# One load cut in two, statistics of two tiles exchanged, and written order lists in place of a planner

## The chip, the core and the metric

The kernel runs on one core of one Trainium2 chip. Its time is device microseconds of one execution; the profile is one execution taken by the hardware profiler. The engines are called as in the profile: PE (TensorE matmuls), PEld (TensorE weight loads), DVE (VectorE), ACT (ScalarE), POOL (GpSimd), SP (SyncE, which here issues the DMAs).

## The reference

`x` is 1 x 2048 x 512, `w1` and `w2` are 512 x 512, `w3` is 512 x 1792, `w4` is 1792 x 512, all bf16.

```python
h  = gelu(layernorm(x) @ w1)
c  = D // 4          # four column groups, moved along the sequence by 1, -1, 2, -2 rows, zeros at the ends
hs = concat(h[0:c] down 1, h[c:2c] up 1, h[2c:3c] down 2, h[3c:] up 2) @ w2
x1 = x + hs
return x1 + gelu(layernorm(x1) @ w3) @ w4
```

## The kernel before, in words

The 2048 rows are 16 tiles of 128 rows. Everything stays in SBUF: `x_sb`, the four weights, the transposed normed rows `xnT`, the first activations `hT`, the second ones `h2T`. Numbers q name a tile and its layer norm: q is t for the first norm, 16 + t for the second.

The steps of one tile have names that the text uses. **Statistics**: either `bnst` and `bnag` on DVE (L432, L434), or `sum` and `ssq` on ACT with small `mean`, `msq`, `vpe` on DVE (L411 to L428); the table `STAT_ACT` says which. The second norm's sum comes out of the DVE instruction that makes x1. **rstd** is on POOL (L439). **norm** (L448, L461, L470, L473) is on the engine that `NORM` says, DVE where it says nothing; on ACT and POOL it needs `nmr` first (L466). Tile 0 is only centered, in two halves `norm0_0` and `norm0_1`; its rstd is applied in the gelu (`gelur0`). **tp**: the transpose, for tiles 0 to 7 of the first norm on PE (L506) with an eviction `ev` (L514), for the rest a transposing DMA on SP's queue (L479). **up1** (w1, L642; tile 0 as `rows0_0` and `rows0_1`, L544, with a transpose `th0` and eviction `evh0` back), **mix** (w2 with the row shifts, L697), **x1** (the residual add, L709 or L713), **up2** (w3, L642, blocks named by their first column group), **gelu** (L657), **down** (w4, L731), **res** (L739), **out_dma** (L742).

PSUM has three pairs of banks, `y_ps`, for up1, up2 and the `ty` and `sa` transposes, and two single banks, `o_ps`, for `mix`, `down`, `th` and the `tp` transposes. A step that takes a bank waits for the reader of the step that had it two steps (pair: three steps) before.

Each engine runs its own instructions in program order. PE's order is written in `SCRIPT`. The order on SP, ACT, DVE and POOL is found when the program is built: `order()` gives each operation a due time, worked back from PE's order with the durations written at each `add`, and `place()` walks through a model of engines and queues and takes on each engine what is ready and due first. `LOADS` fixes the order of the loads. The operations that `place()` starts before `ENTRY` are emitted ahead of the entry barrier.

Nine matmuls on zeros (`warm1`, L756) run while the first loads are under way. Only semaphore waits tie the engines together; `emit` derives them from the operations' reads and writes.

Of the kernel before, what the change touches and what calls it, by code (L numbers as in the profile page):

```python
# [6 lines left out]
P = 128  # L7
# [7 lines left out]
class Op:  # L15


    def __init__(self, name, eng, fn, reads, writes, dur, queue):
        self.name, self.eng, self.fn = name, eng, fn
        self.reads, self.writes = list(reads), list(writes)  # L20
        self.dur, self.queue = dur, queue
        self.idx = 0
        self.descs = 8.0
        self.prio = 1e9
        self.first = None

class Program:

    HOP = {"pe": 200.0, "dve": 155.0, "act": 220.0, "pool": 120.0, "sp": 70.0}
    LOOK = {"dve": 300.0, "act": 300.0}
    DUE = 179877.0
    BEGIN = {"sp": 30.0, "act": 150.0, "pe": 400.0, "dve": 150.0, "pool": 450.0}
    ENTRY = 1900.0
    COLD, RESTART = 4300.0, 800.0
    RING = 150.0
    LAG = {"load": 750, "tp": 350}

    def __init__(self):  # L40
        self.ops = []
        self.lines = []

    def add(self, eng, name, fn, reads=(), writes=(), dur=100.0, queue=None):
        op = Op(name, eng, fn, reads, writes, dur, queue)
        op.idx = len(self.ops)
        self.ops.append(op)
        return op

    def line(self, names):  # L50

        self.lines.append(list(names))

    def order(self):
# [25 lines left out]
        order_only = set()  # L80
        for names in self.lines:
            for a, b in zip(names, names[1:]):
                assert named[a].eng == named[b].eng, (a, b)
                order_only.add((named[a].idx, named[b].idx))
        last = None
        pe_pos = 0
        for op in self.ops:
            if op.eng == "pe":
                if last is not None:
                    preds[op.idx].add(last.idx)  # L90
                last = op
                op.prio = pe_pos
                pe_pos += 1
        order_only = {(a, b) for a, b in order_only if a not in preds[b]}
        for a, b in order_only:
            preds[b].add(a)
        succs = [set() for _ in self.ops]
        for i, d in enumerate(preds):
            for j in d:
                succs[j].add(i)  # L100
        left = [len(s) for s in succs]
        stack = [i for i, n in enumerate(left) if n == 0]
        seen = 0
        while stack:
            i = stack.pop()
            seen += 1
            for j in preds[i]:
                if self.ops[j].eng != "pe":
                    self.ops[j].prio = min(self.ops[j].prio, self.ops[i].prio)
                left[j] -= 1  # L110
                if left[j] == 0:
                    stack.append(j)
        assert seen == len(self.ops), "cycle"
        if self.DUE:

            topo, left = [], [len(d) for d in preds]
            stack = [i for i, n in enumerate(left) if n == 0]
            while stack:
                i = stack.pop()
                topo.append(i)  # L120
                for j in succs[i]:
                    left[j] -= 1
                    if left[j] == 0:
                        stack.append(j)
            due, t = {}, self.DUE
            for op in self.ops:
                if op.eng == "pe" and not op.name.startswith("warm"):
                    due[op.idx] = t
                    t += op.dur
            for i in reversed(topo):  # L130
                op = self.ops[i]
                late = due.get(i, 1e9)
                for j in succs[i]:
                    o = self.ops[j]
                    hop = 70.0 if op.queue else (self.HOP[op.eng] if o.eng != op.eng else 120.0)
                    work = (2300.0 if op.queue == "tp" else op.dur + 1850.0) if op.queue else op.dur
                    late = min(late, o.prio - hop - work)
                op.prio = late
        for op in self.ops:
            op.prio += BIAS.get(op.name, 0.0)  # L140
            if op.first is not None:
                op.prio = op.first
        for names in self.lines:
            for a, b in reversed(list(zip(names, names[1:]))):
                named[a].prio = min(named[a].prio, named[b].prio - 1e-3)

        self.preds = preds
        out = self.place(succs, order_only)
        for a, b in order_only:
            preds[b].discard(a)  # L150
        return out

    def place(self, succs, order_only):

        npend = [len(d) for d in self.preds]
        ready = [0.0] * len(self.ops)
        cands = {e: [] for e in ENGINES}
        for op in self.ops:
            if npend[op.idx] == 0:
                cands[op.eng].append(op)  # L160
        free = dict(self.BEGIN)
        rings = {"sp": [], "act": []}
        fed = {}
        clock = moved = last = turned = self.total = 0.0
        out = []

        def finish(limit):
            nonlocal clock
            while True:
                heads = {e: r[0] for e, r in rings.items() if r}  # L170
                if not heads:
                    return None
                live = [e for e in heads if heads[e][0] <= clock]
                later = min([h[0] for h in heads.values() if h[0] > clock], default=1e18)
                if not live:
                    if later > limit:
                        return None
                    clock = later
                    continue
                first = min(live, key=lambda e: heads[e][1])  # L180
                step = heads[first][1] * len(live)
                ends = clock + step <= min(later, limit)
                if not ends:
                    step = min(later, limit) - clock
                for e in live:
                    heads[e][1] -= step / len(live)
                clock += step
                if ends:
                    return rings[first].pop(0)[2]
                if clock >= limit:  # L190
                    return None

        def release(op, o, at):
            npend[o.idx] -= 1
            if at is not None:
                ready[o.idx] = max(ready[o.idx], at)
            if npend[o.idx] == 0:
                cands[o.eng].append(o)

        def land(op):  # L200
            nonlocal moved, last, turned
            if op.queue == "tp":
                turned = max(clock + 500.0, op.start + 2450.0, last + 500.0, turned + 480.0)
                at = turned + self.LAG["tp"]
            elif op.name.startswith("out"):
                at = clock + 300.0
                self.total = max(self.total, at)
            else:
                moved += op.dur
                at = clock + 600.0 + min(600.0, 0.3 * moved) + (600.0 if op.dur > 1400.0 else 0.0)  # L210
                at += 50.0 if moved <= 1200.0 else self.LAG["load"] - 300.0 if moved <= 4000.0 else self.LAG["load"] if moved <= 11000.0 else self.LAG["load"] + 650.0
            if op.queue != "tp":
                last = max(last, at)
            op.landed = at
            for j in succs[op.idx]:
                if (op.idx, j) not in order_only:
                    release(op, self.ops[j], at + 30.0)

        while len(out) < len(self.ops):
            while True:  # L220
                best = None
                for e in ENGINES:
                    if cands[e]:
                        t = max(free[e], min(ready[o.idx] for o in cands[e]))
                        if best is None or t < best[0]:
                            best = (t, e)
                op = finish(best[0] if best else 1e17)
                if op is None:
                    break
                land(op)  # L230
            t, e = best
            look = self.LOOK.get(e, 1.0)
            op = min((o for o in cands[e] if ready[o.idx] <= t + look), key=lambda o: (o.prio, o.idx))
            cands[e].remove(op)
# [674 lines left out]
```

## Time and profile before

| | |
|---|---|
| three runs | 134.98, 135.43, 135.43 us; median 135.43 |
| span of the profiled execution | 133.7 us (its whole time is not given; the runs lie 1.3 to 1.7 above its span) |
| busy | PE 130.6, PEld 71.8, ACT 56.0, DVE 50.9, POOL 30.9 us |
| chain that ended last | PE 94% of the span, DMA 2%, DVE 2% |
| loads | x0-1 issued at 0.08 us, landed 2.8 later; x2 issued at 0.59, landed 2.6 later |
| transposing DMAs | 24, median 2.5 us to landing, 2.4 to 7.0 |
| waits of DVE for the first load | 2.5 us |

The span runs from the first to the last instruction. A line of the timeline or of a group names engine, line of the code, operation, output and input; "x4" counts instructions; brackets give idle time ahead of the engine and what ended it. In a view by stretches each engine has its busy time, then comes the granted PE clock, the DMA share and GB/s. A matmul's end is modelled, and a few per cent of matmul records are missing.

### The profile page before, as it was taken

What the parts mean: (1) busy time and instruction counts of PE and PEld (TensorE: products, weight loads), DVE (VectorE), ACT (ScalarE), POOL (GpSimd) and SP (SyncE); (2) the same over time, 40 slices, a digit from 0 to 9 for tenths busy, and PEclk for the clock granted to TensorE, in tenths of its full rate; (3) what the DMA queues carried; (4) which work ended last, traced back from release to release, by engine and by line L of the source; (5) the groups of instructions that cost most, each with busy time, mean ns of one, the idle gap of its engine ahead of it and who ended that gap; (6) DMA issues with size and microseconds to landing.
All of it is one profiled execution on the core that took longest, in us unless ns stands there. A gap on an engine that the chain in (4) does not pass through costs nothing.

```text
span 133.7 us, 2004 instructions
## 1 busy us (share of the span) xinstructions
PE 130.6 (98%) x776; PEld 71.8 (54%) x789; DVE 50.9 (38%) x138; ACT 56.0 (42%) x89; POOL 30.9 (23%) x69
## 2 busy tenths in 40 slices
PE   8999999999999999999999999999999999999994
PEld 3488768874488444444444444444444444444464
DVE  1899998887550830052260003322220000232223
ACT  5699998858657155520025553000006663000000
POOL 2447567696544120012022003100000000000000
PEclk9999999999999999999999999999999999999999
DMA  4999966745442991002211000311111000111112
GB/s 134 329 349 401 237 150 95 83 89 107 98 99 49 295 329 40 0 0 43 77 42 39 0 0 0 78 39 44 39 42 37 0 0 0 39 44 39 39 39 78
DMA packets 21305, 12.19 MB, mean 91 GB/s; under 512 B 13872, under 2 KB 20784, under 8 KB 21296
## 3 DMA queue, kind: packets, MB, share of 16 engines
q1 hardware_dynamic: 20864, 11.93, 32.7%
q10 hardware_dynamic: 432, 0.13, 0.4%
q8 instruction: 6, 0.10, 0.3%
q14 instruction: 3, 0.02, 0.1%
HBM read 6.82 MB, written 2.10 MB: 67 GB/s over the span
## 4 chain that ended last, share of the span: by engine, by line
PE 94%; DMA 2%; DVE 2%; issue 1%; SPq 0%
PE y_ps L642 46%; PE o_ps L731 36%; PE o_ps L697 10%; DMA x_sb<-in_x_dram 2%; PE y_ps L506 1%; DVE st L432 1%; PE y_ps L544 1%; DVE xn_buf L448 0%; DVE xn_buf L461 0%; DVE o_sb L739 0%; PE o_ps L610 0%; DVE mv L434 0%; SPq L894 0%
## 5 line engine op out<-in xcount | busy, mean ns | idle before, releaser
L642 PE MATMUL y_ps<-xnT,w_sb 128*128 128x512 bf16 (+2 forms) x421 | 63.6, 308 | 0.2
L642 PEld LDWEIGHTS y_ps<-xnT,w_sb 128*128 128x128 bf16 x424 | 38.4, 98 | 24.6 <-DVE mv L434 0.2
L731 PE MATMUL o_ps<-w_sb,h2T 128*128 128x512 bf16 (+3 forms) x248 | 48.7, 355 | 0.2
L657 ACT ACTIVATE h2T<-y_ps 128x1024 bf16<-128x1024 f32 (+1 forms) x29 | 28.6, 993 | 47.2 <-PE y_ps L642 47.1
L731 PEld LDWEIGHTS o_ps<-w_sb,h2T 128*128 128x128 bf16 x252 | 23.6, 98 | 25.2
L739 DVE TENSOR_TENSOR o_sb<-o_ps,x_sb 128x512 bf16<-128x512 f32 (+3 forms) x18 | 11.4, 632 | 45.7 <-PE o_ps L731 45.7
L439 POOL TENSOR_TENSOR rstd<-mv,neghalf 128x1 f32<-128x1 f32 x20 | 11.1, 553 | 35.1 <-DVE mv L434 30.1
L697 PE MATMUL o_ps<-w_sb,hT 128*128 128x512 bf16 x58 | 14.8, 379 | 0.3
L432 DVE BATCH_NORM_STATS2 st<-x_sb 128x6 f32<-128x512 bf16 x20 | 13.5, 676 | 2.6 <-DMA x_sb<-in_x_dram 2.5
L713 DVE TENSOR_TENSOR x_sb<-o_ps,x_sb 128x512 bf16<-128x512 f32 x10 | 6.8, 677 | 14.8 <-PE o_ps L697 14.8
L439 POOL TENSOR_TENSOR rstd<-vpe,neghalf 128x1 f32<-128x1 f32 x12 | 6.7, 558 | 15.6 <-DVE vpe L428 15.5
L473 POOL TENSOR_SCALAR xn_buf<-x_sb,rstd,nmr 128x512 bf16<-128x512 bf16 x12 | 9.2, 764 | 1.0 <-DVE nmr L466 0.4
L657 ACT ACTIVATE hT<-y_ps 128x512 bf16<-128x512 f32 (+1 forms) x10 | 8.1, 806 | 3.1 <-PE y_ps L642 2.9
L697 PEld LDWEIGHTS o_ps<-w_sb,hT 128*128 128x128 bf16 x64 | 6.1, 98 | 5.7
L709 DVE SCALAR_TENSOR_TENSOR x_sb<-o_ps,x_sb 128x512 bf16<-128x512 f32 x6 | 4.1, 681 | 12.1 <-PE o_ps L697 12.1
L416 ACT ACTIVATE junk<-x_sb 128x512 bf16<-128x512 bf16 x12 | 7.5, 622 | 2.1 <-DVE x_sb L709 2.0
L461 DVE TENSOR_SCALAR xn_buf<-x_sb,mv,rstd 128x512 bf16<-128x512 bf16 x13 | 6.1, 471 | 2.7 <-POOL rstd L439 2.0
L470 ACT ACTIVATE xn_buf<-x_sb,nmr,rstd 128x512 bf16<-128x512 bf16 x6 | 4.9, 813 | 0.5 <-POOL nmr L466 0.4
L756 PE MATMUL o_ps<-zeros 128*128 128x512 bf16 x9 | 4.0, 631 | 0.4 <-DVE zeros L363 0.4
L411 ACT ACTIVATE junk<-x_sb 128x512 bf16<-128x512 bf16 x6 | 3.7, 624 | 1.2 <-DMA x_sb<-in_x_dram 1.2
L434 DVE BATCH_NORM_AGGREGATE mv<-st 128x2 f32<-128x9 f32 x20 | 3.8, 192 | 0.3
L506 PE MATMUL y_ps<-ident,xn_buf 128*128 128x128 bf16 x32 | 3.4, 236 | 0.2 <-DVE xn_buf L461 0.2
(34 smaller groups left out, 28.7 us busy)
## 6 DMA issues: line engine op xcount, KB each, us to landing
out_dram<-o_sb SPq DMA_DIRECT2D x15, 128.0 KB, 1.7
w_sb<-in_w_dram SPq DMA_DIRECT2D x1, 1792.0 KB, 10.9
w_sb<-in_w_dram SPq DMA_DIRECT2D x2, 896.0 KB, 6.2
x_sb<-in_x_dram SPq DMA_DIRECT2D x4, 256.0 KB, 3.6
w_sb<-in_w_dram SPq DMA_DIRECT2D x4, 256.0 KB, 4.3
x_sb<-in_x_dram SPq DMA_DIRECT2D x5, 128.0 KB, 4.5
x_sb<-in_x_dram SPq DMA_DIRECT2D x1, 384.0 KB, 5.7
xnT<-xn_buf SPq DMA_TRANSPOSE x24, 2.5
```

Source lines behind the costliest of these rows:

```text
L416: (lambda d: (lambda e: e.activation(d, src, ACT_F.Square, accum_out=sums[:, q, 1:2])))(junk[:, b, :]),
L432: pg.add("dve", f"bnst{q}", lambda e: e.bn_stats(st9[:, q, 0:6], src), reads=rs, writes=[(("st", q), 0)], dur=605)
L439: lambda e: e.tensor_tensor(col(rstd), var, neghalf[:], ALU.pow),
L461: lambda e: e.tensor_scalar(dst, src, mv[:, q, 0:1], rstd[:, q : q + 1], ALU.subtract, ALU.mult),
L470: f = lambda e: e.activation(dst, src, ACT_F.Identity, bias=nmr[:, q : q + 1], scale=rstd[:, q : q + 1])
L473: f = lambda e: e.tensor_scalar(dst, src, rstd[:, q : q + 1], nmr[:, q : q + 1], ALU.mult, ALU.add)
L642: ins = e.matmul(y_ps[:, p, W * i : W * (i + 1)], wsb[:, dc, P * fc : P * (fc + 1)], src[:, dc, P * t0 : P * t0 + W], start=(dc == 0), sto ...
L657: (lambda d, s: (lambda e: e.activation(d, s, ACT_F.Gelu_apprx_tanh)))(dst, ysrc),
L697: ins = e.matmul(dst, hT[:, j, c0 : c0 + P], w2_sb[:, j, :], start=(j == order[0]), stop=(j == order[-1]))
L713: f = lambda e: e.tensor_tensor(x1_sb[:, t, :], dst, x_sb[:, t, :], ALU.add)
L731: ins = e.matmul(dst, h2T[:, fc, P * t : P * (t + 1)], w4_sb[:, fc, cs], start=(fc == 0), stop=(fc == FC - 1))
L739: (lambda d, c: (lambda e: e.tensor_tensor(o_sb[:, oi, c], d, x1_sb[:, t, c], ALU.add)))(dst, cs),
```

## The change

The planner (`place()`, due times, durations, `BIAS`) goes; the order of SP, ACT, DVE and POOL stands in `ORDER`, one list for each, and `AHEAD` names what is emitted ahead of the entry barrier. `SCRIPT` can name single blocks of up1 and up2. The order itself is other than before: x0 is loaded alone and x1 and x2 together; tile 0's statistics are bnst and bnag on DVE, tile 2's are sum and ssq on ACT; other tiles change engine in `NORM`, `EVAC`, `STAT_ACT`, `NMR` and `HEV`; up2 blocks stand between mix, up1 and down steps; the transposes of tiles 1, 6 and 7 use single banks.

```diff
 GROUPS = {1: (1, 1, 1, 1, 1, 2, 1, 2, 2, 4), 2: (2, 2, 4, 4, 4)}
-NORM = {5: "act", 6: "pool", 7: "act", 9: "pool", 10: "pool", 11: "act", 12: "act", 15: "pool", 18: "act", 19: "pool", 20: "act", 21: "pool", 23: "pool", 25: "pool", 26: "pool", 28: "pool", 30: "pool", 31: "pool"}
-EVAC = {1: "both", 2: "dve", 4: "dve", 5: "dve", 6: "both", 7: "dve", 8: "dve", ...}
-STAT_ACT = (0, 5, 7, 9, 10, 12, 19, 21, 23, 24, 25, 31)
+NORM = {4: "pool", 6: "pool", 9: "act", 10: "act", 18: "act", 19: "pool", 20: "act", 25: "pool", 26: "act", 29: "pool", 31: "act"}
+EVAC = {0: "dve", 1: "dve", 2: "both", 3: "act", 4: "dve", 5: "act", 6: "dve", 7: "dve"}
+STAT_ACT = (2, 7, 9, 10, 12, 16, 17, 18, 19, 21, 25, 28)
-HEV = {0: "dve", ...}
+HEV = {0: "act"}
-NMR = {0: "pool", 1: "pool", 3: "pool", 5: "pool", ...}
+NMR = {4: "pool", 6: "pool", 18: "pool", 20: "pool", 25: "pool", 26: "pool"}
 LOADS = """
-x0-1 x2 tp2 w1a w1b x3 x4-5 w2b w2a tp5 x6 tp6 x7 x8-10 tp4 w3 x12-13 tp0 x11 tp17 x14-15 tp26 tp5 w4a tp3
-w4b
+x0 x1-2 w1a w1b x3 x4-5 w2b w2a x6 x7 x8-10 w3 x12-13 x11 x14-15 w4a w4b
 """
+AHEAD = "zeros trip0 trip1 neghalf ident0 epsc pad0 ident1 pad1 warm_gelu warm1 dma_x0 dma_x1 dma_w1a dma_w1b".split()
 SCRIPT = """
-warm:9 sa:0 sb:0 ty:1 ra:0 rb:0 ty:2 up1:1 th:0 up1:2 mix:0 ty:3 mix:1 ty:4 up1:3 ty:5 up1:4 ty:6 mix:2
-up1:5 ty:7 mix:3 up1:6 mix:5 mix:4 up2:0 up1:7 mix:6 up1:8 mix:7-8 up1:9 mix:10 mix:9 up2:1 mix:13 mix:11
-up2:2 mix:14 down:2 down:1 down:0 mix:12 up2:3 mix:15 down:3 down:5 down:7 down:4 down:6 down:10 up2:4
-down:8 down:11 down:9 down:12-15
+warm:9 sa:0 sb:0 ra:0 tp:1 rb:0 ty:2 up1:1.0 th:0 up1:2.0 ty:3 mix:0 mix:1 ty:4 up1:3.0 up1:4.0 tp:6 ty:5
+mix:2 tp:7 up1:5.0 mix:3 up1:6.0 mix:5 mix:4 mix:6 up2:0.0 up2:0.4 up2:0.8 up1:7.0 up1:8.0 mix:7 mix:8
+up2:0.12 mix:10 mix:9 up1:9.0 up2:1.0 up1:9.2 up2:1.4 mix:13 mix:11 up2:1.8 mix:12 up2:2.0 up2:1.12 up2:2.2
+up2:2.4 down:1 up2:2.6 mix:14 up2:2.8 up2:2.10 down:0 mix:15 up2:3.0 up2:3.2 up2:3.4 down:2 up2:2.12 down:3
...
 """
+ORDER = {
+    "sp": """
+dma_x0 dma_x1 dma_w1a dma_w1b dma_x3 dma_x4 dma_w2b dma_w2a dma_x6 dma_x7 dma_x8 dma_x11 dma_w3 dma_x12 tp16
+tp17 dma_x14 tp8 tp9 tp10 tp11 tp18 tp13 tp12 tp14 tp15 tp19 tp23 tp22 tp21 tp20 dma_w4b dma_w4a tp28 tp25
+tp26 out_dma1_0 tp24 tp30 tp27 out_dma3_0 tp31 out_dma5_0 ...
+""",
+    "act": """
+warm_gelu sum2 ssq2 gelur0 ev2act gelu1_1_0 evh0 gelu1_2_0 ev3 ssq7 sum7 sum9 ssq16 gelu1_3_0 ssq17 ev5 ssq9
+gelu1_4_0 sum10 ssq10 gelu1_5_0 ssq18 ssq19 gelu1_6_0 norm9 norm18 ssq21 norm10 sum12 ssq12 gelu2_0_0
...
+""",
+    "dve": """
+zeros bnst0 bnag0 bnst1 norm0_0 bnag1 norm0_1 msq2 vpe2 ev0_0 norm1 ev0_1 norm2 ev1 bnst3 ev2dve bnag3 bnst4
+norm3 bnag4 bnst5 bnst6 bnag6 x1_0 bnag5 ev4 msq7 x1_1 mean16 vpe7 norm5 msq16 mean17 msq9 vpe16 ev6 norm7
+msq17 vpe17 norm16 x1_2 ev7 norm17 mean18 vpe9 bnst8 msq10 msq18 bnag8 x1_3 norm8 nmr9 mean19 vpe10 msq19
+vpe19 vpe18 x1_5 nmr10 x1_4 nmr19 mean21 bnst20 x1_6 bnag20 bnst22 bnst11 bnag22 bnag11 bnst13 norm11 msq21
...
+""",
+    "pool": """
+trip0 trip1 neghalf ident0 epsc pad0 ident1 pad1 rstd0 rstd1 rstd2 rstd3 rstd4 nmr4 norm4 rstd6 rstd5 nmr6
+norm6 rstd7 rstd16 rstd17 rstd9 rstd8 rstd10 rstd18 rstd19 nmr18 norm19 ...
+""",
+}
```

For comparison, the order that the planner gave SP was: x0-1, x2, w1a, w1b, x3, x4-5, w2b, w2a, x6, x7, x8-10, w3, x12-13, x11, tp16, tp17, x14-15, tp9, tp8, tp10, tp11, tp12, tp13, tp14, tp15, tp19, tp18, tp21, tp20, tp22, tp23, tp24, tp26, w4a, w4b, tp25, tp27, tp29, tp30, out_dma2, out_dma1, out_dma0, tp28, tp31 and the other writes; and DVE's began with zeros, bnst1, bnag1, norm0_0, norm0_1, bnst2, norm1, bnag2, msq0, vpe0, norm2, ev1dve, bnst3, ev2.

## The prediction

> **What bounds the kernel now.** I read the busy shares first, then TensorE (PE) by stretch of the span, then its timeline, then the DMA queues.
>
> ```profile
> PE 130.6 (98%) x776; PEld 71.8 (54%) x789; DVE 50.9 (38%) x138; ACT 56.0 (42%) x89; POOL 30.9 (23%) x69
> 0.00:5.12 5.12, 4.45 (x13) 1.66 (x14) 2.32 (x9) 3.24 (x8) 1.55 (x13) 1.00 0.62 206
> 5.12:20.00 14.88, 14.72 (x160) 11.24 (x164) 13.75 (x47) 13.73 (x35) 9.34 (x19) 1.00 0.92 288
> 20.00:34.00 14.00, 13.95 (x106) 10.29 (x106) 11.57 (x39) 11.05 (x19) 10.12 (x21) 1.00 0.57 92
> 64.00:132.00 68.00, 67.61 (x337) 32.22 (x341) 12.97 (x25) 15.06 (x16) 3.16 (x6) 1.00 0.11 32
> ```
>
> The first line is the page's, the others the view by stretches: length, then busy time of PE, PEld, DVE, ACT, POOL. From 5.12 us on PE is full. Its leftover of some hundredths is matmul records missing from the trace (a step of four shows three). The timeline has one true PE wait after the warm-up:
>
> ```profile
> 4.24 0.63 PE L506 MATMUL y_ps<-ident,xn_buf 128*128 128x128 bf16 x4
> 5.12 0.49 PE L506 MATMUL y_ps<-ident,xn_buf 128*128 128x128 bf16 x4 [0.25 <-DVE xn_buf L461]
> 31.47 3.62 PE L642 MATMUL y_ps<-xnT,w_sb 128*128 128x512 bf16 x16
> ```
>
> The third line is up1_9, the first block that needs tp15, the last DMA transpose of layer 1; it began on time. From 5.12 to 20 us DVE and ACT are over nine tenths busy too: little room there.
>
> The matmul work is the same after the change: same tiles transposed on PE (0 to 7), same groups, same nine warm-ups. So the end moves only by when dense PE work begins and by new PE waits. The last matmuls, their eviction (0.26) and the final write stay. The span is 133.7; the median 135.43 lies 1.7 above it (the three runs 1.3 to 1.7), and that part is left alone. I add the sum to both.
>
> **The change, part by part.**
>
> *Head.* x0 alone is 128 KB instead of 256. The two load rows, x0-1 and then x2:
>
> ```profile
> DMA to landing us min/median/max: 2.8/2.8/2.8
> DMA to landing us min/median/max: 2.6/2.6/2.6
> ```
>
> Issued at 0.08 and 0.59, they land at 2.85 and 3.16: 128 KB more cost 0.30. So x0 lands at about 2.53 (estimate; between 2.3 and 2.85), and x1-2, the same bytes in total, at 3.16. DVE then runs bnst0 (0.69) to 3.22, bnag0 to 3.45, and, because its list says so, bnst1 (starts 3.36, to 4.05) before norm0_0. Before, norm0_0 began 0.84 after the landing (3.71); now about 1.43 after it: 3.96, to 4.21. So the 0.32 won by the load is given back by the second bnst. PE's warm-up ends at 4.24 in any case. tp0_0 runs at 4.27, tp0_1 at 4.54; ev0_0, now on DVE behind msq2 and vpe2, runs 4.73 to 5.01; rows0_0 starts at 5.07, tp1 (norm1 to 5.43) at 5.5, rows0_1 at 5.73, tp2 at 6.16, up1_1 at 6.4 to 6.5. Before, up1_1 began at 6.54. Head: -0.1, bounds -0.25 and +0.2. It can't be much better: PE's order needs the warm-up, a transpose, an eviction and rows0_0 one after the other, and that alone reaches 5.0.
>
> *Statistics and norms moved.* DVE still has 20 bnst and ACT 12 ssq. POOL norms fall from 12 to 5, DVE gains 7 (0.41 each, 2.9 in all), ACT keeps 6. None of it is on the path unless a norm is late for its transpose. Three are, each followed by its own rows. norm4 now goes to POOL: bnag4 ends 8.45, rstd4 (0.55) 9.09, nmr4 (0.26) 9.45, norm4 (0.76) 10.31, tp4 10.41; PE is free at 10.36: 0.06. norm6 waits for POOL behind norm4, rstd6, rstd5: ends 12.46, tp6 12.56, PE free at 12.43: 0.13. norm5 on DVE meets that POOL norm. What that costs stands in this pair:
>
> ```profile
> 25.42 0.76 POOL L473 TENSOR_SCALAR xn_buf<-x_sb,rstd,nmr 128x512 bf16<-128x512 bf16 x1
> 25.53 0.80 DVE L461 TENSOR_SCALAR xn_buf<-x_sb,mv,rstd 128x512 bf16<-128x512 bf16 x1 [0.24 <-POOL rstd L439]
> ```
>
> The DVE norm took 0.80 instead of 0.41, ending 0.14 after POOL's. vpe7, queued ahead of norm5, would be held likewise (vpe12 took 0.53 instead of 0.16 beside norm10), which pushes norm5 from 12.39 to 12.79 and costs tp5 0.06; msq16 to norm7 behind it shift too, and tp7 has 0.06 to spare. Then mix6, moved ahead of up2_0, needs the bank that x1_5 frees (19.41) when mix4 is just done (19.39): 0.08. Sum 0.33; bounds 0 (all inside my reading error of 0.1 each) and 0.7 (each 0.1 worse).
>
> *PE order.* up2_0 is split: three blocks (1.745 each) before up1_7 and up1_8, the last (0.87) after mix8. mix6 goes first. up1_9_0 came at 31.47; now the same steps stand ahead of it in another order, and mix10 and mix9 (0.86 each) besides: 31.47 + 1.73 + 0.2 = 33.4. up2_3 (due 63.6) needs tp27, which in SP's list stands behind out_dma1, tp24 and tp30: mix14 ends 56.4, x1_14, res1, bnst30, bnag30, rstd30, norm30 to 59.5, tp30 59.7, tp27 61.0, landed 63.5: room 0.1, cost 0 (bounds 0 and 0.3).
>
> *SP's list.* tp18 is put ahead of tp13, tp12, tp14 and tp15, and norm10 comes later: ACT does gelu1_6, norm9, norm18 (waits for nmr18 until 20.2), ssq21, then norm10 to 22.47; tp10 is issued at 22.57 (before: 21.12). tp11 waits for norm11 (24.24): 24.34. Then tp18, 13, 12, 14, 15 at SP's pace of 1.31 each: tp15 at 30.89, landed 2.45 later at 33.34. Due 33.4: room 0.05. Before, tp15 landed at 31.16, due 31.47: room 0.3, with a block of 1.0 already paid. That block is the row the forecast rests on:
>
> ```profile
> GB/s 0 3 148 225 215 212 69 2 0 109 20 176 210 201 176 35 0 0 0 7 9 9 10 10 12 0 60 188 217 218 173 19 0 0 0 137 224 215 215 82
> q8 instruction: 1, 0.02, 1.5%
> DMA to landing us min/median/max: 4.2/4.2/4.2
> L479 SPq DMA_TRANSPOSE xnT<-xn_buf x1: 2272/2272/2272, 23.7 to 23.7; - x1
> DMA to landing us min/median/max: 2.5/2.5/2.5
> ```
>
> The first two lines are the DMA view of 22 to 28 us: one 16 KB instruction packet (queue 8; 1.5% of 16 engines for 6 us is 1.4 us, and it stands at 23.43 to 24.90), and from 24.3 to 25.9 nothing else moves. The others are SP's transposes one by one: tp11, issued 22.36, landed after 4.2; tp12's issue took 2.27 instead of 1.27, so tp13 came at 26.01 instead of 25.00; from then on 2.5 again. The six such packets start when PE and PEld have done 256, 424, 669, 933, 1167 and 1419 instructions, mostly some 250 apart, so I take them as PE's. In the new PE order the second one comes at the same instruction, mix6 and 33 matmuls of up2_0 on: 20.3 + 33 x 0.109 = 23.9, with tp10 in flight and the queue without a gap until tp15. Price: up to 1.0, all of it visible, since the room is 0.05: up1_8 (needs tp11, due 27.3) would wait some 0.4, up1_9 the rest. The average packet is shorter (0.3% of 16 engines over the span, over six: 1.07), so bounds are 0 and 1.3; I take 0.8.
>
> [...]
>
> *Rest.* x11 ahead of w3 (128 KB) delays w3 by about 0.3: due at 20.3, landed 16.5 before. The dropped planner and durations issue nothing. The set issued ahead of the entry barrier has the same members. SP still issues 24 transposes; w4 stands behind tp20 at about 40 and is needed at 51. Cost 0; w4's cover is some 3 us.
>
> Sum: -0.1 + 0.33 + 0.8 = +1.0: span 134.7, time 136.4 (+0.75%).
>
> **Rivals.** *The packet costs nothing here* (it falls between two transposes, or is only as long as the shortest): then +0.2, 135.6, not slower by what can be told. For it: the packet of 40.4 to 41.7 stood beside one transpose (issued 40.79, landed after 2.5) and cost it nothing. Against: that transpose was alone; from 22.6 to 33.3 there will be no gap between them. It decides if the delay is below 0.4. [...] *A second choke*: a further packet on the transposes (queue 14 moved two of 8 KB at 20.1 and 21.1, where tp9 and tp8 took 4.0 and 3.9) or up2_3 on tp27: +0.5 more, 136.9. *Faster*: x0's landing shortens the start and no wait is real: rows0_0 at 5.0 and dense from there gives -0.25, 135.2. Over 0.5% (0.68) it would have to start some 0.4 before ev0_0 can be done; I see no way. That the lists don't do what they say is hardly possible: they are the program order.
>
> **Numbers.** 0.5% (0.68 us) is about what a measurement of this kernel can tell from no change; the runs before differ by 0.45. Chances: forecast 0.52 (of which 0.08 has a delay so small that the total stays under 0.68), harmless packet 0.30, second choke 0.13, start gain 0.05 (0.03 of it beyond 0.5%, for what I can't see). Slower 0.44 + 0.13 = 0.57; same 0.08 + 0.30 + 0.02 = 0.4; faster 0.03. The range takes the harmless case with 0.3 of spread below, and the second choke's middle: 135.3 to 136.9; the forecast's own is 135.9 to 136.8.
>
> **What would show it.** Right: in the new PE timeline gaps before up1_8 and up1_9 (27 to 35 us) ended by a transpose, one SP transpose taking over 2 us to issue near 24, and up1_1 at 6.4 to 6.5. Wrong: PE dense through 27 to 35 with all transposes landing in 2.5 (then 135.6); or first dense work before 5.0.

## The result, and the profile after

The changed kernel took 137.24 us (median of six executions, 136.5 to 137.75) beside 135.43: 1.0134 times the kernel before (95% interval 1.0109 to 1.016). The forecast was 136.4, at most 136.9: the direction held, the time lies above the range. Its profiled execution took 137.26, with a span of 135.4; before, the span was 133.7. In all that follows "outside the span" means an execution's time less its span. One execution of e4_packet_early, two of e9_room and one of e12_before_loads (its profiled one) were slow, above all the others of their kernel; times, spans and ratios leave them out, and that profile is not read.

The busy line of the page, and PE by stretch (length, then busy time of PE, PEld, DVE, ACT, POOL):

```profile
PE 131.6 (97%) x776; PEld 71.3 (53%) x789; DVE 50.7 (37%) x147; ACT 54.2 (40%) x86; POOL 24.3 (18%) x55
5.12:20.00 14.88, 14.51 (x153) 10.56 (x156) 13.59 (x53) 12.72 (x32) 8.55 (x16) 1.00 0.81 279
20.00:34.00 14.00, 13.95 (x107) 10.40 (x108) 11.87 (x36) 9.66 (x16) 7.11 (x14) 1.00 0.46 86
34.00:36.00 2.00, 1.50 (x8) 0.56 (x7) 1.97 (x7) 0.00 (x0) 0.61 (x1) 1.00 0.39 78
64.00:132.00 68.00, 67.68 (x319) 31.47 (x323) 11.25 (x18) 15.74 (x16) 0.55 (x1) 1.00 0.11 31
```

POOL has 14 instructions fewer (55 for 69); that will matter at the very end. PE is full from 64 us on, as before. What it lost lies ahead of 20 us and between 34 and 36. PE's timeline at these places (start, length, engine, line, operation; in brackets the idle time ahead and what ended it):

```profile
4.35 0.59 PE L344 MATMUL y_ps<-ident,xn_buf 128*128 128x128 bf16 x4
5.27 1.01 PE L381 MATMUL y_ps<-w_sb,xnT 128*128 128x512 bf16 x2 [0.34 <-DVE xnT L352]
7.03 1.07 PE L477 MATMUL y_ps<-xnT,w_sb 128*128 128x128 bf16 x16
34.88 5.36 PE L477 MATMUL y_ps<-xnT,w_sb 128*128 128x512 bf16 x31 [0.49 <-DMA xnT<-xn_buf]
```

The first three are tp0, rows0_0 and up1_1. Up1_1 came at 7.03; before, its row was

```profile
6.54 1.06 PE L642 MATMUL y_ps<-xnT,w_sb 128*128 128x128 bf16 x16
```

The fourth is up1_9, waiting for tp15: 34.88, before 31.47 with 1.73 of mix steps less ahead of it. The chain of waits (start, length, piece) passes through that wait:

```profile
30.96 0.70 DVE x_sb L547
31.66 0.51 SPq L317
32.22 2.53 DMA xnT<-xn_buf
34.88 4.07 PE y_ps L477 x26
```

SP's transposes fill their queue up to 32.22, the last lands 2.5 later, and PE stands. How the queue came to be late is seen in the DMA view of 24 to 30 us and in tp11's own row:

```profile
GB/s 0 20 184 225 215 188 42 0 0 109 0 0 0 0 61 140 205 222 177 68 26 24 5 0 1 0 0 0 123 224 215 217 93 4 0 0 12 174 222 220
q8 instruction: 1, 0.02, 1.0%
L317 SPq DMA_TRANSPOSE xnT<-xn_buf x1: 1849/1849/1849, 25.1 to 25.1; - x1
```

The instruction packet (queue 8) ran from 25.48 to 26.48. Behind the packet's own column (the 109) the GB/s row is empty up to 26.1; tp11's issue took 1.85 instead of 1.27, and its landing 3.0 instead of 2.5. PE's spacing shows 0.13 of wait before up1_8 and 0.66 before up1_9.

### The profile page after: what moved, and what is told of

It reads as the page before. It is cut to its first block, busy times and chain, and to the rows that moved or that the text cites. A ratio compares the mean times of both kernels' runs of the same rounds, so it can differ in the third digit from the quotient of the medians.

```text
span 135.4 us, 1992 instructions
## 1 busy us (share of the span) xinstructions
PE 131.6 (97%) x776; PEld 71.3 (53%) x789; DVE 50.7 (37%) x147; ACT 54.2 (40%) x86; POOL 24.3 (18%) x55
## 4 chain that ended last, share of the span: by engine, by line
PE 91%; DMA 4%; issue 1%; ACT 1%; DVE 1%; SPq 1%; DVEq 0%
PE y_ps L477 45%; PE o_ps L565 36%; PE o_ps L531 8%; DMA x_sb<-in_x_dram 2%; DMA xnT<-xn_buf 2%; PE y_ps L381 1%; PE y_ps L344 1%; PE o_ps L344 1%; ACT junk L250 1%; DVE x_sb L547 1%; ACT junk L255 0%; SPq L317 0%; SPq L224 0%; DVE o_sb L573 0%; PE o_ps L446 0%
## 5 line engine op out<-in xcount | busy, mean ns | idle before, releaser
L477 PE MATMUL y_ps<-xnT,w_sb 128*128 128x512 bf16 (+2 forms) x417 | 64.4, 307 | 0.9 <-DMA xnT<-xn_buf 0.5
L565 PE MATMUL o_ps<-w_sb,h2T 128*128 128x512 bf16 (+3 forms) x250 | 49.8, 355 | 0.1
L492 ACT ACTIVATE h2T<-y_ps 128x1024 bf16<-128x1024 f32 (+1 forms) x29 | 27.8, 991 | 48.0 <-PE y_ps L477 48.0
L547 DVE TENSOR_TENSOR x_sb<-o_ps,x_sb 128x512 bf16<-128x512 f32 x9 | 6.1, 685 | 17.3 <-PE o_ps L531 17.2
L299 DVE TENSOR_SCALAR xn_buf<-x_sb,mv,rstd 128x512 bf16<-128x512 bf16 x20 | 8.0, 404 | 2.9 <-POOL rstd L278 2.9
L255 ACT ACTIVATE junk<-x_sb 128x512 bf16<-128x512 bf16 x12 | 7.5, 623 | 0.8 <-DVE x_sb L543 0.8
L543 DVE SCALAR_TENSOR_TENSOR x_sb<-o_ps,x_sb 128x512 bf16<-128x512 f32 x7 | 4.8, 685 | 0.2 <-PE o_ps L531 0.2
L311 POOL TENSOR_SCALAR xn_buf<-x_sb,rstd,nmr 128x512 bf16<-128x512 bf16 x5 | 3.8, 763 | 1.0 <-DVE nmr L304 0.4
L250 ACT ACTIVATE junk<-x_sb 128x512 bf16<-128x512 bf16 x5 | 3.1, 624 | 1.6 <-DMA x_sb<-in_x_dram 1.6
L267 DVE SCALAR_TENSOR_TENSOR vpe<-sums,mv 128x1 f32<-128x1 f32 x12 | 2.1, 182 | 2.4 <-ACT junk L255 2.3
```

Source lines behind the costliest of these rows:

```text
L255: (lambda d: (lambda e: e.activation(d, src, ACT_F.Square, accum_out=sums[:, q, 1:2])))(junk[:, b, :]),
L299: lambda e: e.tensor_scalar(dst, src, mv[:, q, 0:1], rstd[:, q : q + 1], ALU.subtract, ALU.mult),
L477: ins = e.matmul(y_ps[:, p, W * i : W * (i + 1)], wsb[:, dc, P * fc : P * (fc + 1)], src[:, dc, P * t0 : P * t0 + W], start=(dc == 0), sto ...
L492: (lambda d, s: (lambda e: e.activation(d, s, ACT_F.Gelu_apprx_tanh)))(dst, ysrc),
L543: f = lambda e: e.scalar_tensor_tensor(x1_sb[:, t, :], dst, 1.0, x_sb[:, t, :], ALU.mult, ALU.add, accum_out=sums[:, NT + t, 0:1])
L547: f = lambda e: e.tensor_tensor(x1_sb[:, t, :], dst, x_sb[:, t, :], ALU.add)
```

## The experiments

Times are medians; the ratio is to the kernel before on the same chip, with its 95% interval; "span" is the median of the executions' spans, "outside" their range outside the span. The kernel before had 135.42 to 135.50 beside all of them, with spans of 134.1 (134.2 beside e5 to e8) and 1.3 to 1.4 outside.

| run | kernel | time | ratio | span | outside |
|---|---|---|---|---|---|
| (first) | after | 137.24 | 1.0134 [1.0109, 1.016] | 135.4 | 1.50 to 2.01 |
| e11_after_again | after | 136.65 | 1.0082 [1.0067, 1.0097] | 135.15 | 1.47 to 1.53 |
| e1_tp18_late | after | 136.85 | 1.0109 [1.0085, 1.0132] | 135.2 | 1.49 to 1.91 |
| e4_packet_early | after | 136.67 | 1.0095 [1.0062, 1.0129] | 135.2 | 1.46 to 2.05 |
| e5_pool_spare | after | 136.65 | 1.0084 [1.0058, 1.011] | 135.3 | 1.33 to 1.38 |
| e9_room | after | 135.80 | 1.0027 [1.0014, 1.0041] | 134.45 | 1.30 to 1.37 |
| e8_norm46 | after | 136.36 | 1.0076 [1.0051, 1.01] | 134.8 | 1.51 to 1.57 |
| e2_head_back | after | 136.76 | 1.0099 [1.0071, 1.0128] | 135.2 | 1.45 to 1.91 |
| e16_head_back_room | after | 135.83 | 1.0033 [1.0018, 1.0048] | 134.5 | 1.29 to 1.40 |
| e3_fill | after | 136.49 | 1.0071 [1.0045, 1.0098] | 134.6 | 1.46 to 2.01 |
| e13_norm0_first | after | 136.73 | 1.0107 [1.0085, 1.0128] | 135.2 | 1.45 to 2.01 |
| e17_start_free | after | 136.95 | 1.0119 [1.0095, 1.0142] | 135.6 | 1.31 to 1.41 |
| e7_all | after | 136.79 | 1.0106 [1.0074, 1.0139] | 135.25 | 1.52 to 1.60 |
| e10_room_all | after | 136.07 | 1.0042 [1.0029, 1.0054] | 134.55 | 1.47 to 1.60 |
| e14_norm0_room | after | 135.83 | 1.0038 [1.0022, 1.0055] | 134.3 | 1.48 to 1.58 |
| e18_all_mended | after | 136.55 | 1.0091 [1.0072, 1.0111] | 135.0 | 1.50 to 1.57 |
| e6_before_fill | before | 135.34 | 0.9994 [0.9978, 1.001] | 133.95 | 1.30 to 1.41 |
| e12_before_loads | before | 136.20 | 1.0055 [1.0036, 1.0073] | 134.9 | 1.30 to 1.37 |
| e15_before_loads_again | before | 135.88 | 1.003 [1.0018, 1.0042] | 134.5 | 1.29 to 1.38 |

The second column names the kernel that was edited. No version beat the kernel before.

### The packet and the transposes: e1, e4, e9

e1 moves tp18 behind the transposes of layer 1:

```diff
-tp17 dma_x14 tp8 tp9 tp10 tp11 tp18 tp13 tp12 tp14 tp15 tp19
+tp17 dma_x14 tp8 tp9 tp10 tp11 tp13 tp12 tp14 tp15 tp18 tp19
```

> One move in SP's list of the changed kernel: tp18 goes from between tp11 and tp13 to behind tp15. Theory (tp15 has no room, and the blocked issue of tp11 shows through it): tp15 lands 1.31 us earlier, the 0.66 us before up1_9 goes, up2_1 waits some 0.1 for tp19 instead, time 0.5 to 0.6 us below the changed kernel (about 136.7). Rival (the place of the wait just moves to up2_1, because tp18 and tp19 are as late as tp15 was): no change within 0.2.

up1_9 no longer waited, but the queue was as late as before and the next reader paid, up2_1, on a transpose further on:

```profile
34.12 1.89 PE L477 MATMUL y_ps<-xnT,w_sb 128*128 128x512 bf16 x8
36.54 3.63 PE L477 MATMUL y_ps<-xnT,w_sb 128*128 128x256 bf16 x24 [0.52 <-DMA xnT<-xn_buf]
```

The span did not move (135.2): the rival was right. tp18's place is not the cause; it only chose who waits.

e4 moves the packet. Its place seems to go by the count of PE's instructions: where the six packets of queue 8 begin, PE and PEld have started 247, 437, 728, 916, 1166 and 1421 of them in after, 256, 424, 669, 933, 1167 and 1419 in before. So the nine warm-up matmuls of 512 columns become 36 of 128, the same work in 54 more PE and PEld instructions:

```diff
-            rows = zeros[:].unsqueeze(1).to_broadcast([P, 4, P])
+            rows = zeros[:]
...
-                for _ in range(n):
-                    ins = e.matmul(o_ps[:, b, :], zeros[:], rows, start=True, stop=True)
+                for _ in range(4 * n):
+                    ins = e.matmul(o_ps[:, b, 0:P], zeros[:], rows, start=True, stop=True)
```

> The nine 128x512 matmuls on zeros become 36 of 128x128: same time, but 54 more TensorE instructions ahead of everything, so the second 16 KB instruction packet (25.48 to 26.48 in the changed kernel) should come some 27 matmuls, 2.9 us, earlier, at about 22.5, where no transposing DMA moves data. Theory (the packet is what blocks tp11's issue for 0.57): tp11's issue takes 1.27 again, tp15 lands 0.6 earlier, the wait before up1_9 falls from 0.66 to about 0.1, time 0.5 to 0.6 below the changed kernel (about 136.7). Rival (tp11 is held by something of its own, such as its input or the queue): the packet moves and tp11's issue stays near 1.85, no change in time.

The six packets came at 12.64, 21.04, 37.96, 65.12, 86.72 and 114.64 us (after: 14.49, 25.48, 46.9, 66.12, 93.2, 120.8): earlier, by 1.0 to 8.9. tp11, issued at 24.8, took 1.19 and landed after 2.7, and up1_9 came without a bracket:

```profile
L317 SPq DMA_TRANSPOSE xnT<-xn_buf x1: 1192/1192/1192, 24.8 to 24.8; - x1
33.96 6.23 PE L477 MATMUL y_ps<-xnT,w_sb 128*128 128x512 bf16 x40
```

In that profile the waits before up1_8 and up1_9 fell from 0.79 to 0.12, at a span of 134.5. A rival falls with it: an 8 KB packet of queue 14 also ran beside the transposes (from 26.17 in after), and in e4 it ran at the same place (25.89) while they kept their pace. The spans of e4's other executions scatter from 134.4 to 135.5, and the median time is not lower than e5's; so e4 shows whose packet it is and what it does, and not the gain in time.

e9 leaves the packet where it is and gives the transposes room, that is, issues them earlier than PE's need of them asks (with 14 spare POOL memsets, below):

```diff
-gelu1_6_0 norm9 norm18 ssq21 norm10 sum12
+gelu1_6_0 norm9 norm10 ssq21 norm18 sum12
...
-nmr19 mean21 bnst20 x1_6 bnag20 bnst22 bnst11 bnag22 bnag11 bnst13 norm11 msq21
+nmr19 mean21 bnst11 bnst20 bnag11 x1_6 bnag20 norm11 bnst22 bnag22 bnst13 msq21
...
-nmr18 norm19 rstd20 rstd11 nmr20
+nmr18 norm19 rstd11 rstd20 nmr20
```

> The kernel after, with 14 spare memsets at the end of POOL's list (by the earlier run with them alone the time outside the span goes back to 1.35) and room for the last transposes of layer 1: ACT does norm10 before norm18, DVE does bnst11, bnag11 and norm11 earlier, POOL rstd11 before rstd20, so that tp10 to tp15 can be issued about 1.4 us earlier. Theory (the wait of 0.79 before up1_8 and up1_9 is there because the packet meets transposes that have no room): tp11 is issued near 23.6, tp15 lands at 33.3 to 33.9 instead of 34.75, up1_9 waits at most 0.3, the span is 134.6 to 134.8, the time about 136.0 (0.7 us below the run with the spare memsets alone). Rival (some other transposing DMA or packet then sets the end, as when tp18 alone was moved): the span stays at 135.2 to 135.5, the time at 136.6.

tp11 was issued at 23.72. The packet (25.61) met it all the same: it landed after 4.1, and tp18's issue behind it took 2.3. tp15 landed at 34.07, and PE did not wait:

```profile
32.48 1.89 PE L534 MATMUL o_ps<-w_sb,hT 128*128 128x512 bf16 x8
34.20 6.02 PE L480 MATMUL y_ps<-xnT,w_sb 128*128 128x512 bf16 x37
```

The span's median fell from e5's 135.3 to 134.45, the time from 136.65 to 135.80. So the packet is a price only where the transposes have no room, and here that price is about 0.8 in time. In the profiles of kernels without that room it varies: the two waits add up to 0.79 in after, 0.57 in e11, 0.52 in e3 and 1.03 in e5.

### Outside the span: e5, e11

```diff
-nmr26 rstd30 rstd31
+nmr26 rstd30 rstd31 spare0 spare1 ... spare13
```

> Fourteen small POOL memsets on a column of their own are added at the end of POOL's list in the changed kernel; nothing reads them and POOL is idle there. In the runs so far the time outside the span is 1.31 to 1.39 us for the kernel before and 1.45 to 2.05 (near 1.5 or near 1.95) for the changed one, whose trace has an 8 KB instruction packet on queue 14 1.8 us after the last instruction; the kernel before has its third such packet at 40.8. The built programs have 78 POOL instructions before, 64 after. Theory (with 14 fewer POOL instructions a block boundary of POOL's stream falls behind the kernel's end, and the end waits for the packet): the packet goes back inside the span, time outside the span 1.31 to 1.4, span unchanged (135.4), time 0.3 to 0.5 below the changed kernel (about 136.8). Rival (the time outside the span has another cause, such as DVE's or ACT's stream): it stays 1.5 to 2.0 and the time stays.

The spare operations are 14 memsets of one column at the end of POOL's list: they do no work that anybody needs. All six executions had 1.33 to 1.38 outside the span, as the kernel before; after had 1.5 or 1.9 to 2.0, nothing between. What stands there is seen in the DMA view from 134 us on, after's first, then e5's (start of the row at 134, 0.125 us a column):

```profile
GB/s 0 3 200 123 3 0 117 80 0 0 0 0 0 0 0 0 0 0 0 0 0 0 0 0 0 66 0 0 0 0 0 0 0 0 0 0 0 0 0 0
q14 instruction: 1, 0.01, 0.4%
```

```profile
GB/s 0 0 120 192 16 0 61 125 11 0 0 0 0 0 0 0 0 0 0 0 0 0 0 0 0 0 0 0 0 0 0 0 0 0 0 0 0 0 0 0
```

After fetches an 8 KB instruction packet on queue 14 at 137.15, 1.75 us behind its last instruction. With the memsets that third packet moved to 48.23, where it lies under other work; before has it at 40.79. Of the profiled executions only after's and e3's have a packet behind the end, and these two had 1.86 and 1.98 outside; the other profiled executions of after and its versions without the memsets had 1.49 to 1.54. So with 14 POOL instructions fewer a fetch is left for the end of the program (137.15 in after, beside 48.23 with the memsets), and where it is seen there the time outside is some 0.6 longer. That the executions with 1.5 have the same fetch, only not recorded, is not shown: the memsets took their 0.15 away too, but e7, e10, e14 and e18, whose third packet lies at 47 to 48 us, have 1.5 all the same.

> The kernel after, unchanged, on the chip of these runs. By what its earlier runs showed: time 137.2 +- 0.3, spans with a median of 135.4, time outside the span between 1.5 and 2.0 and in two clusters. Rival (the difference to the other kernels is one of chips or of hours): 136.7 or less, and 1.35 outside the span.

Between theory and rival: the time was 136.65, the spans 134.9 to 135.3, and all six had 1.5 outside. Of after's twelve executions eight had 1.5 outside and four 1.9 or 2.0. The first measurement had all four; that is two thirds of its distance to this one (0.38 by the medians, out of 0.59).

### The start: e2, e3, e6, e12, e15, e13, e17, e16

e2 puts the start of before into after, with DVE's list, POOL's rstd order and AHEAD to match:

```diff
-x0 x1-2 w1a
+x0-1 x2 w1a
-STAT_ACT = (2, 7, 9, ...)
+STAT_ACT = (0, 7, 9, ...)
-warm:9 sa:0 sb:0 ra:0 tp:1 rb:0 ty:2
+warm:9 sa:0 sb:0 tp:1 ra:0 rb:0 ty:2
```

> The start alone is put back in the changed kernel: loads x0-1 and x2, tile 0's statistics on ACT (sum0, ssq0), tile 1 and 2 on DVE, ev0_0 and ev0_1 on ACT, tp1 ahead of rows0. Theory A (the new start costs 0.5: ev0_0 stands behind ssq2 and vpe2, and TensorE's matmuls stay at half pace until 6.2 instead of 5.35): up1_1 starts near 6.5 instead of 7.03, time 0.5 below the changed kernel (about 136.7). Rival B (when the pace doubles is chance from run to run and not tied to the start): 0.1 to 0.2 below only.

136.76, span 135.2: no lower than after's 135.15 to 135.4 by anything that can be told, where half a microsecond stood in the profile. In e2's profile up1_1 came at 6.75, but up1_8 and up1_9 then waited 0.96 instead of 0.79: what the start wins, the late transposes take back. With them out of the way (e16, the old start and e9's room) it can be read:

> The kernel with room for the transposes and spare POOL memsets, and the start of the kernel before (x0-1 and x2, tile 0's statistics on ACT, its evictions on ACT, tile 1's transpose ahead of rows0_0). Theory (start, small waits, packet and the part outside the span are all): only the small waits of some 0.36 are left over the kernel before: span median 134.3 to 134.5, time 135.6 to 135.8. Rival (the old start doesn't pay in the new order): 135.9 or more, as with room and the new start.

135.83 and a span of 134.5, the same as e9's 135.80 and 134.45, and 0.4 above before's: by time between theory and rival, by span the theory's. So on average the new start costs nothing that can be told in this order, though 0.44 lie between the profiles of e9 and e16 at up1_1 (7.14 and 6.70); in that profile of e9 the second load landed later than in any other with this start (3.83).

A part of such differences is the pace of the matmuls. In after's profile the steps from rows0_0's two matmuls to what follows each were 0.38 and 0.43, from about 6.2 us on they are 0.22. e3 puts one warm-up matmul into the gap before rows0_0, e6 does the same to the kernel before:

```diff
-warm:9 sa:0 sb:0 ra:0 tp:1
+warm:9 sa:0 sb:0 warm:1 ra:0 tp:1
```

> One more matmul on zeros (128x512) is put between tp0_1 and rows0_0 of the changed kernel, in the 0.5 us in which TensorE stands idle there. Theory A (the idle time is why matmuls stay at half pace until 6.2): the pace doubles at about 5.4, rows0_0 takes 0.43 instead of 0.8, time 0.3 to 0.4 below the changed kernel (about 136.9). Rival B (the moment is chance, or counts from the launch): no change within 0.1.

> The kernel before with one more matmul on zeros between tp0_1 and tp1, in its idle 0.45 us; POOL's first constants come in another order, all else as before. Theory A (TensorE's idle time ahead of the first dense step makes the doubling of its pace late in some runs, in both kernels): spans less spread than 133.7 to 134.7, median span 133.7 to 133.9, time 0.2 to 0.4 below the kernel before. Rival B (the moment is chance that idle time doesn't touch, and the 0.75 that the fill won in the changed kernel was something else): same time within 0.1.

e3 had full pace at rows0_0 (5.30) and up1_1 at 6.64, and its span was 134.6. But in its profile tp0's last two matmuls and the filling matmul start 0.07 and 0.06 apart (0.11 in e13, at half pace): the pace was up at 4.68, before the filling had run, so the filling did not bring it; e6 changed nothing; in e10 rows0_0's first step was 0.38 in spite of the filling; and e1 and e13 had full pace at rows0_0 without it. Where a trace has a record of the granted clock from early on, it agrees with the pace: the record begins, at full clock, at 6.17 us in after, 6.36 in e11, 6.38 in e8, 5.88 in e10 and 3.92 in e1, all with the start of after, and at 5.37 in before. (The clock column of the views shows 1.00 ahead of that as well, where the trace has no record.) So the step to full pace lay anywhere from 3.9 to 6.4 us in these profiles; what sets its moment is not shown. In e3's profile, 0.6 below after's, 0.39 are at up1_1 and 0.27 at the transposes; what the lower median comes from stays open.

e12 does the edit of the title's first half alone, in the kernel before; PE's order stays, and the planner makes the other engines' lists anew:

```diff
-x0-1 x2 tp2 w1a
+x0 x1-2 tp2 w1a
-STAT_ACT = (0, 5, 7, ...)
+STAT_ACT = (2, 5, 7, ...)
-EVAC = {1: "both", ...}
+EVAC = {0: "dve", 1: "both", ...}
```

> The kernel before with the first words of the change alone: x0 as a load of its own, x1 and x2 in the next, statistics of tile 0 on DVE, of tile 2 on ACT, the eviction ev0 on DVE; PE's order and the planner stay. Theory (the loss comes from the order lists, not from this): the start moves by -0.1 to +0.3, no new wait after 6 us, 1.35 outside the span, time 135.3 to 135.8. Rival (the loads and statistics themselves cost the loss): 136.2 or more, with the first dense PE work 0.8 later.

> The kernel before with the new loads, statistics and eviction of the start, unchanged from its earlier run. Theory (tile 0's norm waits for the second load, and the evictions of tile 0 and norm1 stand one after the other on DVE): x1-2 lands at 3.2 to 3.5, tile 0's transpose starts 1.25 later, up1_1 at 7.2 to 7.5 beside 6.54 before, no other wait; span median 135.0, time 136.3. Rival (the loss is elsewhere): up1_1 before 6.9 and a wait after 10 us.

136.20 and, repeated, 135.88: by the medians the edit alone costs 0.4 to 0.8 there, with PE's order unchanged. Why it costs that in the order of before and nothing visible in that of after (e9 beside e16) is open. The first theory fell. The repeat's trace shows how (PE, then DVE):

```profile
4.61 0.59 PE L506 MATMUL y_ps<-ident,xn_buf 128*128 128x128 bf16 x4
7.01 1.06 PE L642 MATMUL y_ps<-xnT,w_sb 128*128 128x128 bf16 x16
```

```profile
3.38 0.69 DVE L432 BATCH_NORM_STATS2 st<-x_sb 128x6 f32<-128x512 bf16 x1 [0.23 <-DMA x_sb<-in_x_dram]
4.10 0.20 DVE L434 BATCH_NORM_AGGREGATE mv<-st 128x2 f32<-128x9 f32 x1
4.22 0.44 DVE L448 TENSOR_SCALAR xn_buf<-x_sb,mv 128x256 bf16<-128x256 bf16 x2
```

Tile 0's norm (L448) stands behind tile 1's statistics, which wait for x1-2 (3.35). up1_1 came at 7.01, 0.47 later than before; the expectation said 7.2 to 7.5, and no other wait, but mix0 waited 0.24 at 9.2.

The changed kernel has the same queueing: in the ten profiles of kernels with its start, x1-2 landed at 3.16 to 3.83, and tp0 began 1.05 after that landing or at 4.24 (the end of the warm-up), whichever was later. Two kernels take it away. e13 moves the norm, e17 (with the spare memsets) the eviction too:

```diff
-zeros bnst0 bnag0 bnst1 norm0_0 bnag1 norm0_1 msq2 vpe2 ev0_0 norm1 ev0_1 norm2
+zeros bnst0 bnag0 norm0_0 norm0_1 bnst1 bnag1 msq2 vpe2 ev0_0 norm1 ev0_1 norm2     (e13)
+zeros bnst0 bnag0 norm0_0 norm0_1 bnst1 bnag1 ev0_0 ev0_1 norm1 msq2 vpe2 norm2     (e17)
```

> The kernel after with one move on DVE's list: norm0_0 and norm0_1 ahead of bnst1 and bnag1, so that tile 0's first transpose needs x0 alone. Theory (the start is late because norm0_0 stands behind the second load): norm0_0 ends near 3.4, tile 0's transpose starts at 4.24 with the end of the warm-up whatever x1-2 does, ev0_0 no later than 4.9, rows0_0 at 5.0 to 5.15 (5.27 to 5.81 in the profiles so far); span and time 0.1 to 0.3 lower than the kernel after: 136.4 to 136.6 beside 136.65 to 137.2. Rival (the late step of the matmul pace is what costs, not the load): rows0_0 earlier, but up1_1 still at 6.8 to 7.2, and time unchanged.

tp0 came at 4.24, and rows0_0 at 5.29 all the same, the span unchanged. DVE's timeline shows the next queueing: vpe2 waits for ACT's squares of tile 2, and ev0_0 stands behind it:

```profile
4.79 0.16 DVE L267 SCALAR_TENSOR_TENSOR vpe<-sums,mv 128x1 f32<-128x1 f32 x1 [0.21 <-ACT junk L255]
4.86 0.28 DVE L352 COPY xnT<-y_ps 128x256 bf16<-128x256 bf16 x1
```

```profile
5.29 0.59 PE L381 MATMUL y_ps<-w_sb,xnT 128*128 128x512 bf16 x2 [0.42 <-DVE xnT L352]
```

That last line, beside after's of 5.27 with 1.01, is also the pace: the same two matmuls at the same time, 0.4 apart at their end.

> The kernel after with spare POOL memsets and DVE's list begun with bnst0 bnag0 norm0_0 norm0_1 bnst1 bnag1 ev0_0 ev0_1 norm1 msq2 vpe2, so that neither tile 0's norm nor its eviction stands behind the second load. Theory (those two queueings are the start term): tile 0's transpose at 4.24, ev0_0 at 4.5 to 4.55, rows0_0 at 4.85 to 4.95 instead of 5.14 to 5.81; tile 1's transpose and rows0_1 then wait for norm1 and for w1's second half (landed 5.1 to 6.4), so that half of it or more is left: span 0.2 to 0.4 below the run with spare memsets alone (median 135.3), 134.9 to 135.1, time 136.3 to 136.45 beside 136.65. Rival (the second half of w1 sets the start, and the pace): rows0_0 earlier, up1_1 at 6.7 or later, time 136.6 or more.

The miss is clear: 136.95, span 135.6, worse than without the edit. rows0_0 came at 5.07, but now vpe2 was late (5.78), hence rstd2 and norm2, and tp2 waited, in DVE's and PE's timelines:

```profile
6.60 0.41 DVE L302 TENSOR_SCALAR xn_buf<-x_sb,mv,rstd 128x512 bf16<-128x512 bf16 x1 [0.66 <-POOL rstd L281]
```

```profile
7.07 0.40 PE L347 MATMUL y_ps<-ident,xn_buf 128*128 128x128 bf16 x4 [0.35 <-DVE xn_buf L302]
```

So neither place of vpe2 that was tried is good: early it holds back tile 0's eviction, late it holds back norm2. A place between, behind ev0_1 and ahead of norm1, was not tried. In the kernel before it was tile 0 whose statistics came by way of ACT, and tile 0's rstd is used only in the gelu; the exchange put the slower way on a tile whose norm PE waits for.

### The small waits: e8

norm4 and norm6 go back to DVE:

```diff
-NORM = {4: "pool", 6: "pool", 9: "act", ...}
+NORM = {9: "act", ...}
-bnst5 bnst6 bnag6 x1_0 bnag5 ev4 msq7 x1_1
+bnst5 bnst6 norm4 bnag6 x1_0 bnag5 ev4 msq7 norm6 x1_1
```

> In the changed kernel norm4 and norm6 go from POOL to DVE (no nmr for them, norm4 behind bnst6, norm6 ahead of x1_1); the rest of the lists stays. Theory (these two and the DVE work that norm6 holds are the waits of 0.09 at tp6 and 0.10 at tp5): both waits go, 0.1 to 0.2 below the changed kernel, which the timing alone can hardly tell; the waits in the trace decide. Rival (DVE becomes late by the 0.8 us of two more norms): tp7, mix2 or mix3 wait instead, no gain or a loss of up to 0.3.

The wait before tp6 went, the one before tp5 grew from 0.10 to 0.18; the median of the spans fell to 134.8, more than the 0.1 that the waits show. Why is open. Outside the span it has 1.51 to 1.57 in every execution, and so have all kernels with this edit, e18 too, which has as many POOL instructions as before; this 0.18 is not explained.

### All together: e7, e10, e14, e18

e7 joins e3, e4, e5 and e8; e10 has e9, e3 and e8; e14 has e9, e8 and e13; e18 has e9, e8, e17 and 18 memsets.

> The changed kernel with everything that theory blames put right at once: the filling matmul ahead of rows0, 36 small warm-up matmuls (which move the instruction packet ahead of tp10), fourteen spare POOL memsets, and norm4 and norm6 on DVE instead of POOL. Theory (new waits 0.8 at the transposes, 0.35 at tp6, tp5 and mix6, some 0.2 of start, 0.45 outside the span, nothing else): span 134.0 to 134.3, 1.35 around it, time 135.4 to 135.7, the kernel before within 0.3. Rival (something else in the new order costs too): 136.0 or more.

136.79, the rival's number, though not by a new cost: with e4's warm-ups a later packet moved onto tp24, tp30 and tp27, which have as little room, and up2_3 waited:

```profile
q8 instruction: 1, 0.02, 1.5%
64.94 3.40 PE L480 MATMUL y_ps<-xnT,w_sb 128*128 128x512 bf16 x14 [0.81 <-DMA xnT<-xn_buf]
```

> The kernel with room for the transposes and spare POOL memsets, and besides one 512-column warm-up matmul between the two transposes of tile 0, and norm4 and norm6 on DVE as before the change. Theory (the start, the small waits, the packet and the part outside the span are all there is, and they add): span 134.3 to 134.6, time 135.7 to 135.9, within 0.3% of the kernel before. Rival (what is mended in one place comes back in another, as in the run with all mends but the room): span 135.0 or more, time 136.3 or more.

Between the two: the span (134.55) held the theory's upper end, the time (136.07) did not, because the 0.18 outside came with norm4 and norm6.

> The kernel with room for the transposes, spare POOL memsets, norm4 and norm6 on DVE, and norm0_0 and norm0_1 ahead of bnst1. Theory: the room's 135.89, less 0.2 for the start and 0.1 to 0.2 for the two norms: 135.5 to 135.7, span median 134.2. Rival (as in the run with room and fill, norm4 and norm6 on DVE give nothing back in all, and the start is set by the pace): 135.9 to 136.1.

The span of 134.3 is 0.2 above before's, the lowest of all kernels with the new order; the time, 135.83, lies between theory and rival for the same 0.18. (The expectation counts from 135.89 for e9; its figure in the table is 135.80.)

> The free start, room for the transposes, norm4 and norm6 on DVE, and 18 spare POOL memsets (so many that POOL has as many instructions as in the kernel before). Theory (start, small waits, packet and the part outside the span are all there is): span 134.0 to 134.3, 1.35 outside it, time 135.3 to 135.6, within 0.2% of the kernel before. Rival: 135.8 or more, as the earlier runs with room.

136.55, the rival's number: e17's late vpe2 is in it (up1_1 at 7.40, in e14's profile 7.07).

## Why the prediction was right or wrong

**The part outside the span** ("that part is left alone") is the step that failed. It was put at nothing, on the ground that the last steps of the kernel stay. (The 1.7 given for it is a median time less the span of another execution; each execution of before has 1.3 to 1.4.) It grew by 0.15 in eight and 0.6 in four executions of after, and e5 brought it back with 14 idle memsets. That POOL had 14 instructions fewer stood in the diff; that a program's last instruction packet can lie behind its end, the trace of before couldn't show; after's shows it, at 137.15.

**The head** was mis-sized for the profiled execution: -0.1, bounds -0.25 and +0.2, against +0.49. The steps up to rows0_0 came 0.1 to 0.2 late (x1-2 at 3.30, not 3.16; ev0_0 at 4.84, not 4.73; rows0_0 at 5.27, not 5.07), and 0.4 more is the pace, which was not in the sum. Over all executions it can't be told from nothing in this order (e9 against e16, 134.45 and 134.5), which is inside the bounds. What the working had wrong is the landing of the second load as one number: I saw that bnst1 stood ahead of norm0_0 and that vpe2 stood ahead of ev0_0, and priced both with a load on time, though x1-2 landed anywhere from 3.16 to 3.83. Of a start gain nothing was left: x0 landed even earlier than estimated, 2.27 for 2.53, and nobody could use it.

**The small waits** held: 0.36 in the profile (mix0 0.06, tp6 0.09, tp5 0.10, mix6 0.09, tp3 0.02) for 0.33, with tp4's missing and mix0's not foreseen.

**The packet** held in place (before up1_8 and up1_9) and in cause: e4 moved it and e9 gave it room. Its size held too, 0.79 for 0.8, but so close an agreement is luck: other profiles have 0.52 to 1.03. (In the row read for it, "nothing else moves" is not quite so: from 24.85 to 25.8 us it has 7 to 12 GB/s.) The harmless packet, which had 0.30, did not come: PE itself did not stop beside the packet (busy for all of 25.48 to 26.48), but SP's transposes were held up (tp11's issue took 1.85 instead of 1.27), at a price of about 0.8 in this kernel's time (e5 beside e9).

**The second choke** was not in after: no PE wait past 45 us. e7 showed that it was where the prediction put it, at up2_3 on tp27 with no room, and that it wants a packet there.

The sum for the span, +1.0, stands beside +1.05 (e11) and +1.3 (first measurement) in the medians, and in the profile +1.7: 0.49, 0.36, 0.79. By the medians of the versions, nothing of it is the start (e9 beside e16), 0.85 the packet (e5 beside e9), and 0.4 is left where the start is the old one and the transposes have room (e16 beside before), about the small waits. The part outside the span decided whether the time fell into the range: the repeat, e11, had 0.15 more outside in every execution and lies inside, at 136.65; the first measurement had 0.6 more in four of six and lies above, at 137.24.

## What to carry to other kernels

Look whether a DMA queue that is issued without a gap has room at its end: here it had none for one instruction packet (1.00 us long in after), and PE waited 0.79; moving one transfer (e1), or the packet (e7), only changed who waits, while 1.3 us of earlier issue (tp11 at 23.72 in e9, 25.06 in after) took the wait away. When a load is split, look at which operation in the in-order list of the engine stands behind the second half: the early landing is worth only what doesn't stand behind the late one. And before an engine is relieved of instructions, compare the time outside the span too.

## What I had not expected of the hardware

Fourteen memsets that nobody reads made the program 0.15 to 0.6 us shorter outside its span, and the 8 KB fetch that one profile has behind the end lay at 48 us with them. The packets on queue 8 moved with PE's count of instructions: 54 more of them brought the six packets 1.0 to 8.9 us earlier. And the step to the full matmul pace came at 3.9 us in one profile (3.92 in e1) and at 6.4 in another with the same start (6.38 in e8); e13 and e14, whose rows0_0 came at 5.29 and 5.31, had up1_1 at 6.63 and 7.07 with nothing waiting in between.
